# Transforms of block 1 on split operands, no idle transposes, the last product closed by token tile, and a new order with 912 pieces on another engine

## The chip, the cores and the metric

The kernel runs on one core of one Trainium2 chip. The metric is the device time of one execution in microseconds (us), as the median of several runs. TensorE (PE) multiplies; its weight loads are shown as an engine of their own (PEld). VectorE (DVE), ScalarE (ACT) and GpSimd (POOL) do the elementwise work, and SyncE (SP) issues every DMA of this kernel, one after the other in the order of the program.

## The reference

Two layers of the same two parts, on 2048 tokens of 1024 channels, with a hidden width of 3584:

```python
def _A_ref(q, k, v, shift_k, ssm_k, ssm_D):
    k_shift = sum(k_pad[:, t:t + S] * shift_k[:, ks - 1 - t] for t in range(ks))   # ks = 4
    kv = k_shift * v
    y = irfft(rfft(kv, 2 * S) * rfft(ssm_k, 2 * S))[:S]     # causal convolution, 2048 long, per channel
    return q * (y + kv * ssm_D)

def _B_ref(x, w1, b1, w2, b2):
    h = relu(x @ w1 + b1)
    return (h * h) @ w2 + b2

x = q
for _ in range(2):
    x = x + _A_ref(layernorm(x), k, v, shift_k, ssm_k, ssm_D)
    x = x + _B_ref(layernorm(x), w1, b1, w2, b2)
```

k, v and the filters are the same in both layers. So the convolution y is computed once, kept in device memory and used twice.

## The kernel before, in words

**Tiles.** The tokens are cut into four blocks of 512 (block 0 to 3), a block into four token tiles of 128; the 1024 channels are eight groups of 128. The unit of work is one layer of one block. The eight units run in the order (layer, block) = (0,0), (1,0), (0,1), (0,2), (0,3), (1,1), (1,3), (1,2), and the last four are taken two at a time as a "joint" product with seven partial products in place of eight.

**The large matmuls.** w1, relu squared and w2 make most of TensorE's work. An f32 operand is split in two halves of type fp32r: the high half is a cast by ScalarE, the low half a subtraction (operand minus high half) by VectorE or GpSimd. A product is then three matmuls (`mm3`): high by high, high by low, low by high. The weights stream from device memory: raw rows (`wr`, or `fv` and `jr` tiles), their split (`whl`, `jr`), and for weights that are used again the split form is stored once (`wd_...`) and loaded as it is.

**The convolution.** Blocks of 256 tokens are transformed with tables of cosines (`plain`, 128 by 128 pieces, and their split forms `fh`, `fl`, `ih`, `il`). Block 0's is done ahead of everything else (`first_block`, about the first 116 us). Those of blocks 1 to 3 run in the background of the first four units, as three generators that are advanced at each step of the large matmuls:

- `x_stream` shifts and multiplies K and V (`fwd_kv`), transposes and transforms the result (`fwd_x`), and writes it to device memory as `xd`;
- `g_stream` transforms the filter's rows (`fwd_g`), which come from `ssmR`, and writes `gd`;
- `prod_stream` loads both (`cx`, `cg`), multiplies them (`mult`: `cp<-cx,cg`, in pieces of 128x256 or 128x128), reduces them over the blocks (`red`: `sm<-cp`, VectorE), combines the sums (`fold`, `butterfly`: `sm<-sm`), transforms back (`fin` or `fin_plain`: results in a bank `pt`) and stores `yd`.

A block's `yd` is read when the unit of that block is prepared. For a block up to `PLAIN` the transforms are plain f32 matmuls on the whole operand; beyond it they are `mm3` on halves:

```python
        if sb <= PLAIN:                                        # fwd_x
            xt = mkfx([P, T])
            A.copy(xt, o)
        else:
            hi = mkfx([P, T], F32R)
            lo = mkfx([P, T], F32R)
            A.copy(hi, o)
            yield
            V.tensor_sub(lo, o, hi.bitcast(F32))
```

`fwd_g` does the same with the filter's rows; before, for block 1, its matmul reads the loaded tile `raw` (`fg`) directly. The inverse of block 1 takes one group of 64 channels at a time (`fin_plain`, four matmuls of 128 columns each), that of blocks 2 and 3 two groups together (`fin`: halves `yh` and `yl`, twelve matmuls of 256 columns).

**What sets the order.** Every engine call goes onto a `Tape` first. A unit of the tape is one call, or a run of TensorE calls into the same result tile; `cut(True)` starts a unit that holds all TensorE calls of a step of the large matmuls. `Tape.order` reads the table `ORDERED`, run lengths and jumps that give a permutation of all units, and `Tape.play` issues them in that order. So the recorded order of the functions above is not what runs, and each engine follows its own part of the permutation strictly. All instructions issued this way have one line in the profile: L310, in `play`. Memory is handed out in rings (`fg` 3 tiles, `fx` 4, `fk` 2, `cp` 3, `cx` and `cg` 2, `sm` 2; result banks `p1` 2, `p2` 4, `pt` 2).

**Idle transposes.** `fill(o, n)` issues n transposes of the identity into a bank whose contents are then overwritten; 40 stand at the program's start. Three further places do so: the last channel group of block 0's filter, the first transposes of block 0's tokens, and the transposes behind the normalisation between the first two units.

**The end.** The last partial product of the last joint unit runs over 14 rows p of weights; each row multiplies all four token tiles, into the banks that the names `p_...` and `pt` show at the end of the program. `j_evict` adds each bank to the accumulator (`fg<-pt,fg` and the like) and `j_store` writes it out.

Of the kernel before, what the change touches and what calls it, by code (L numbers as in the profile page):

```python
# [22 lines left out]
P = 128  # L23
# [24 lines left out]
TAIL = 0.1  # L48
LAG_RED = 2
# [25 lines left out]
PLAIN = 1  # L75
FILL = (16, 12, 4)
# [197 lines left out]
class Tape:  # L274
# [20 lines left out]
    def order(self):  # L295
        got, at = [], 0
        for t in ORDERED.split():
            n, sign, jump = re.fullmatch(r"(\d+)([-+]?)(\d*)", t).groups()
            got += range(at, at + int(n))
            at += int(n) + int(sign + (jump or "0"))  # L300
        assert sorted(got) == list(range(len(self.units)))
        return [(i, self.units[i][0]) for i in got]

    def play(self):
        def real(x):
# [2285 lines left out]
```

## Time and profile before

| | us |
|---|---|
| runs | 2574.89, 2571.48, 2575.93 |
| median | 2574.89 |
| the profiled execution's own time | 2572.81 |
| its span, first to last instruction | 2570.9 |
| TensorE busy | 2554.1 |
| weight loads (beside TensorE) | 2149.0 |
| VectorE busy | 1936.2 |
| ScalarE busy | 1139.5 |
| GpSimd busy | 1021.9 |

The granted TensorE clock is 1.000 of full speed. The program has 12184 TensorE records; a plain f32 matmul leaves two of them. All sums are made against the profiled execution's own time; the 1.9 us between it and its span lie before the first and behind the last instruction.

How to read it: a busy line gives, for each engine, the time in which it had an instruction at work. A wait is idle time of one engine ahead of an instruction, with the engine or DMA that ended it behind the arrow. A window is a stretch of the span, with each engine's busy time in it. In a timeline a row has the start, the duration, the engine, the operation with result and operands, and their shapes; an entry with x6 is six instructions of the same kind in a row, its duration that of all of them; a wait ahead of it stands in brackets at the row's end.

### The profile page before, as it was taken

What the parts mean: (1) busy time and instruction counts of PE and PEld (TensorE: products, weight loads), DVE (VectorE), ACT (ScalarE), POOL (GpSimd) and SP (SyncE); (2) the same over time, 40 slices, a digit from 0 to 9 for tenths busy, and PEclk for the clock granted to TensorE, in tenths of its full rate; (3) what the DMA queues carried; (4) which work ended last, traced back from release to release, by engine and by line L of the source; (5) the groups of instructions that cost most, each with busy time, mean ns of one, the idle gap of its engine ahead of it and who ended that gap; (6) DMA issues with size and microseconds to landing.
All of it is one profiled execution on the core that took longest, in us unless ns stands there. A gap on an engine that the chain in (4) does not pass through costs nothing.

```text
span 2570.9 us, 36794 instructions
## 1 busy us (share of the span) xinstructions
PE 2554.1 (99%) x12184; PEld 2149.0 (84%) x12184; DVE 1936.2 (75%) x3053; ACT 1139.5 (44%) x2020; POOL 1021.9 (40%) x1194
## 2 busy tenths in 40 slices
PE   9999999999999999999999999999999999999999
PEld 8988888988888888888888888888888888888887
DVE  8877998788888787878889767885778576755553
ACT  4454344534434333253322565663434566653332
POOL 4547786477573987738889100000300000003000
PEclk9999999999999999999999999999999999999999
DMA  8799999899999999899899879999988576679682
GB/s 283 262 338 336 325 302 317 323 338 381 353 329 366 339 377 337 309 305 369 336 401 371 274 264 318 329 341 383 341 301 295 169 244 225 228 266 376 212 289 82
DMA packets 405328, 792.82 MB, mean 308 GB/s; under 512 B 47505, under 2 KB 150545, under 8 KB 405138
## 3 DMA queue, kind: packets, MB, share of 16 engines
q1 hardware_dynamic: 405138, 790.47, 87.6%
q8 instruction: 96, 1.57, 0.2%
q14 instruction: 94, 0.77, 0.1%
HBM read 583.22 MB, written 207.09 MB: 307 GB/s over the span
## 4 chain that ended last, share of the span: by engine, by line
PE 90%; DMA 4%; DVE 3%; POOL 1%; issue 1%; SPq 1%; ACT 0%; DVEq 0%; POOLq 0%; ACTq 0%
PE p L310 80%; PE pt L310 11%; DMA cg<-gd 1%; DMA wd_m<-whl 1%; POOL cp L310 1%; SPq L310 1%; DVE xl L310 1%; DMA whl<-wd_m 0%; DVE whl L310 0%; DMA jr<-w 0%; DMA jr<-wd_m 0%; DMA fg<-ssmR 0%; DMA gd<-fg 0%; DMA wr<-w 0%; DVE fg L310 0%
## 5 line engine op out<-in xcount | busy, mean ns | idle before, releaser
L310 POOL TENSOR_TENSOR cp<-cx,cg 128x256 f32<-128x256 f32 (+1 forms) x864 | 683.6, 829 | 258.4 <-DVE sm L310 154.0
L310 PE MATMUL p<-xh,whl 128*128 128x512 f32 (+1 forms) x1864 | 566.2, 380 | 2.3 <-DMA whl<-wd_m 2.3
L310 POOL TENSOR_TENSOR acc<-acc,px 128x512 f32<-128x512 f32 x48 | 70.2, 1478 | 893.5 <-DMA rh<-rd 504.7
L310 PE MATMUL p<-whl,rh 128*128 128x512 f32 x1296 | 403.5, 392 | 0.3 <-DVE acc L310 0.3
L310 PEld LDWEIGHTS p<-xh,whl 128*128 128x128 f32 x1864 | 344.4, 188 | 67.0 <-issue 2.7
L310 DVE TENSOR_TENSOR whl<-wr,whl 128x512 fp32r<-128x512 f32 x387 | 299.7, 780 | 86.6 <-ACT whl L310 85.6
L310 PE MATMUL p<-xl,whl 128*128 128x512 f32 (+1 forms) x932 | 352.4, 378 | 0.1
L310 ACT CAST whl<-wr 128x512 fp32r<-128x512 f32 x405 | 246.1, 618 | 144.9 <-PE p L310 68.1
L310 PEld LDWEIGHTS p<-whl,rh 128*128 128x128 f32 x1296 | 240.2, 188 | 48.3 <-DVE acc L310 0.6
L310 DVE TENSOR_REDUCE sm<-cp 128x128 f32<-128x384 f32 (+5 forms) x288 | 249.2, 874 | 27.3 <-POOL cp L310 27.0
L310 PE MATMUL p<-whl,rl 128*128 128x512 f32 x648 | 252.7, 390 | 0.0
L310 PEld LDWEIGHTS p<-xl,whl 128*128 128x128 f32 x932 | 175.5, 188 | 31.5 <-DVE xl L310 0.3
L310 POOL TENSOR_TENSOR sm<-sm 128x256 f32<-128x256 f32 x192 | 167.8, 880 | 82.3 <-DVE sm L310 78.1
L310 ACT ACTIVATE wr<-p,b1t 128x512 f32<-128x512 f32 x130 | 89.7, 690 | 246.2 <-PE p L310 242.6
L310 DVE TENSOR_TENSOR rl<-wr,rh 128x512 fp32r<-128x512 f32 x112 | 104.2, 930 | 83.7 <-ACT rh L310 77.6
L310 PE MATMUL p<-jr,rh 128*128 128x512 f32 x496 | 154.6, 393 | 0.0
L310 PE MATMUL p<-xh,jr 128*128 128x512 f32 (+1 forms) x472 | 145.4, 379 | 0.0
L310 PEld LDWEIGHTS p<-whl,rl 128*128 128x128 f32 x648 | 121.6, 188 | 25.9
L310 DVE TENSOR_TENSOR acc<-p,acc 128x512 f32<-128x512 f32 x152 | 99.1, 684 | 52.7 <-PE p L310 52.6
L310 PE MATMUL p<-whl,xl 128*128 128x512 f32 x528 | 128.6, 389 | 0.0
L310 PE MATMUL p<-rh,whl 128*128 128x512 f32 x336 | 117.1, 389 | 0.0
L310 PE MATMUL p<-rl,whl 128*128 128x512 f32 x336 | 117.1, 389 | 0.0
(309 smaller groups left out, 5004.3 us busy)
## 6 DMA issues: line engine op xcount, KB each, us to landing
whl<-wd_m SPq DMA_DIRECT2D x231, 512.0 KB, 6.8
wr<-w SPq DMA_DIRECT2D x379, 256.0 KB, 5.7
rh<-rd SPq DMA_DIRECT2D x168, 256.0 KB, 5.5
jr<-wd_m SPq DMA_DIRECT2D x60, 512.0 KB, 6.7
rd<-acc SPq DMA_DIRECT2D x120, 256.0 KB, 4.0
wr<-td SPq DMA_DIRECT2D x112, 256.0 KB, 5.3
wd_m<-whl SPq DMA_DIRECT2D x49, 512.0 KB, 6.8
cx<-xd SPq DMA_DIRECT2D x48, 512.0 KB, 6.6
```

What stands on the lines that cost most here:

```text
L310: getattr(self.engines[e], f)(*map(real, a), **{k: real(x) for k, x in kw.items()})
```

## The change

Five things are edited.

- `PLAIN` is 0, so block 1's transforms take the paths of blocks 2 and 3: x and g on split operands, and the inverse with `fin`. The table's halves (`const_split`) are made ahead of block 1 now, and the number of ticks between two groups of x (`X_TICKS`) is that of the later blocks.
- `FILL` and its three uses are gone; the 40 transposes at the start stay.
- In the last product, the last two rows (`TAIL_ROWS`) are held back and issued by token tile: for each of the four, the six matmuls of both rows.
- `ORDERED` is another permutation.
- A second table, `SWAPPED`, names 912 units that go from VectorE to GpSimd or the other way.

```diff
+TAIL_ROWS = 2
...
-PLAIN = 1
-FILL = (16, 12, 4)
+PLAIN = 0
...
 ORDERED = (
-    "4+1 1-2 1+1 1+1 1-2 1+1 1+2 2+1 1+1 1-2 1+1 4+1 3+1 2-18 1+2 1-5 1+11 1+6 2-5 1+5 2+1 4+1 3+1 1+2 1-14 1-4 1+16 "
...
+SWAPPED = (
+    "31 3 91 6 11 101 16 67 9 42 13 13 19 4 2 23 3 5 40 5 11 29 12 2 13 27 8 4 6 7 25 2 10 10 24 8 5 9 1 6 1 30 13 "
...
         assert sorted(got) == list(range(len(self.units)))
-        return [(i, self.units[i][0]) for i in got]
+        swap, at = {}, 0
+        for n in map(int, SWAPPED.split()):
+            at += n
+            swap[at] = {"V": "G", "G": "V"}[self.units[at][0]]
+        return [(i, swap.get(i, self.units[i][0])) for i in got]
...
             def mmk(e):
-                if c == KT - 1:
-                    fill(o.t, FILL[0])
                 for r in range(2):
...
-                    for x in idle:
-                        fill(x.t, FILL[2])
-                pl.add([("PE", 600)], tr, [(ns[t], kh)], [o, *idle])
+                pl.add([("PE", 600)], tr, [(ns[t], kh)], [o])
...
                     o = ps1()
-                    if tts[n] == 2 and kh == 0:
-                        fill(o, FILL[1])
                     for c in range(4):
...
         elif k == "jb":
+            if i == 0:
+                todo_rows = []
...
-            hi, lo = (J.rt[s - jb_at][1][:, n] for n in range(2))
-            for tt in range(NT):
-                t = slice(tt * P, (tt + 1) * P)
-                mm3(os[tt], hi[:, t], lo[:, t], wh, wl, i == 0 and a in JOPEN, i == NP - 1, a not in JOPEN)
+            todo_rows.append((i, *(J.rt[s - jb_at][1][:, n] for n in range(2)), wh, wl))
+            final = u + 2 == NU and a == JORD[-1] and i >= NP - TAIL_ROWS
+            if not final or i == NP - 1:
+                for tt in range(NT):
+                    t = slice(tt * P, (tt + 1) * P)
+                    for n, hi, lo, wh, wl in todo_rows:
+                        mm3(os[tt], hi[:, t], lo[:, t], wh, wl, n == 0 and a in JOPEN, n == NP - 1, a not in JOPEN)
+                    if final:
+                        tape.cut(True)
+                todo_rows = []
             tape.cut()
```

Counted over the whole program: TensorE's matmuls and transposes go from 11768 to 11896, VectorE's instructions from 3053 to 3183, GpSimd's from 1194 to 1112, ScalarE's from 2018 to 2050, and the DMAs on SP's queue from 2434 to 2426. Of the products `cp<-cx,cg`, 309 of 128x256 and 33 of 128x128 run on VectorE now; 720 and 144 ran on GpSimd before. GpSimd has 105 low halves `whl<-wr,whl` (18 before), 33 of `jr` (6), 44 of `rl<-wr,rh` (none), 52 of `yl<-sm,yh` (none) and 23 of `fg<-fk` (none).

Three places show how the order moves. The first is VectorE in block 0, where the third group of channels is shifted (`p_544` before, `p_539` of the change, towards `fx`), while the tokens' statistics (`mv`) become a scale (`ve`, `sd`, `rs`, `rt`). Before:

```order
L310 SCALAR_TENSOR_TENSOR p_544<-xh,shkt,p_544 128x512 x2
L310 TENSOR_SCALAR ve<-mv_555 128x4
L310 RECIPROCAL rs<-sd 128x4
L310 SCALAR_TENSOR_TENSOR p_544<-xh,shkt,p_544 128x512
L310 TENSOR_TENSOR sg<-p_565,sg 128x2x4x64
L310 TENSOR_TENSOR sx<-p_539,sx 128x2x4x64
L310 TENSOR_TENSOR fx<-p_544,fx 128x512
L310 TENSOR_TENSOR sg<-sg,p_565 128x2x4x64
L310 TENSOR_TENSOR rt<-rs 128x4
```

Of the change:

```order
L438 SCALAR_TENSOR_TENSOR p_539<-xh,shkt,p_539 128x512
L438 TENSOR_TENSOR xl<-xl 128x768
L438 RECIPROCAL rs<-sd 128x4
L438 TENSOR_SCALAR ve<-mv_532 128x4
L438 SCALAR_TENSOR_TENSOR p_539<-xh,shkt,p_539 128x512
L438 TENSOR_TENSOR sg<-sg,p_561 128x2x4x64
L438 SCALAR_TENSOR_TENSOR p_539<-xh,shkt,p_539 128x512
L438 TENSOR_TENSOR sg<-p_561,sg 128x2x4x64
L438 TENSOR_TENSOR fx<-p_539,fx 128x512
L438 TENSOR_TENSOR sx<-p_538,sx 128x2x4x64
```

`fx` stands ahead of the eviction `sx` now, and `rt` and what follows from it are no longer on VectorE but on GpSimd:

```order
L438 TENSOR_TENSOR xl<-sx,sg 128x768
L438 TENSOR_TENSOR whl<-wr,whl 128x512
L438 TENSOR_TENSOR rt<-rs 128x4
L438 TENSOR_TENSOR rt<-rt,ve 128x4
L438 TENSOR_TENSOR rs<-rs,rt 128x4
L438 TENSOR_TENSOR xl<-sx,sg 128x768
```

Those rows are GpSimd's, early in block 0; ahead of them it has low halves of weights, and what moved there are the three operations of four columns.

The second place is TensorE in the first unit, at a transform of block 1's filter (`pt<-fg,...`) between the large matmuls (`p_1412`, `p_1705`, `p_1777`). Before:

```order
L310 MATMUL p_1412<-xl,whl 128x256
L310 MATMUL p_1412<-xh,whl 128x256
L310 MATMUL pt<-fg,yh 128x2x128 x4
L310 MATMUL p_1412<-xh,whl 128x256
L310 MATMUL p_1412<-xl,whl 128x256
```

Of the change:

```order
L438 MATMUL p_1705<-xl,jr 128x512
L438 MATMUL p_1705<-xh,jr 128x512
L438 MATMUL pt<-fg,fh 128x2x128 x2
L438 MATMUL pt<-fg,fl 128x2x128
L438 MATMUL pt<-fg,fh 128x2x128 x2
L438 MATMUL pt<-fg,fl 128x2x128
L438 MATMUL pt<-fg,fh 128x2x128 x2
L438 MATMUL pt<-fg,fl 128x2x128
L438 MATMUL pt<-fg,fh 128x2x128 x2
L438 MATMUL pt<-fg,fl 128x2x128
L438 MATMUL p_1777<-xh,jr 128x512
```

Four plain matmuls on the loaded rows became twelve on their halves, and they stand later: behind the large matmuls of 256 columns (two token tiles at a time), among those of 512.

The third place is TensorE at the program's end (the four token tiles' banks: two with names of their own, two called `pt`; `whl`, `jr` and `cp` are operands of the last rows). Before:

```order
L310 MATMUL p_23154<-jr,cp 128x512 x3
L310 MATMUL p_23158<-jr,cp 128x512 x3
L310 MATMUL pt<-jr,cp 128x512 x6
L310 MATMUL p_23154<-whl,cp 128x512 x3
L310 MATMUL p_23158<-whl,cp 128x512 x3
L310 MATMUL pt<-whl,cp 128x512 x6
L310 MATMUL p_23154<-whl,cp 128x512 x3
L310 MATMUL p_23158<-whl,cp 128x512 x3
L310 MATMUL pt<-whl,cp 128x512 x6
```

Of the change:

```order
L438 MATMUL p_23377<-jr,cp 128x512 x3
L438 MATMUL p_23381<-jr,cp 128x512 x3
L438 MATMUL pt<-jr,cp 128x512 x6
L438 MATMUL p_23377<-whl,cp 128x512 x6
L438 MATMUL p_23381<-whl,cp 128x512 x6
L438 MATMUL pt<-whl,cp 128x512 x12
```

The last two rows of weights go to each token tile together: six matmuls to the first bank, six to the second, twelve to the two banks `pt`.

More of the change, by code (lines that the diff above doesn't have):

```diff
@@ L125 @@
 ORDERED = (
[91 rows of a table removed]
[192 rows of a table added]
+)
+SWAPPED = (
[19 rows of a table added]
 )
@@ L1725, in tail, with tr @@
                 o = bank("p1", 2, ps1)
-                idle = [bank("p2", 4, ps2)] if t == 0 and kh else []
-                def tr(e, kh=kh, o=o, idle=idle):
+                def tr(e, kh=kh, o=o):
                     for c in range(4):
```

300 rows, old and new, of tables (ORDERED, SWAPPED) are left out of this document.

## The prediction

> **What bounds the kernel now.** I read the page's busy line first, then the list of who TensorE (PE) waited for, then the busy time by stage.
>
> ```profile
> span 2570.9 us, 36794 instructions
> ...
> PE 2554.1 (99%) x12184; PEld 2149.0 (84%) x12184; DVE 1936.2 (75%) x3053; ACT 1139.5 (44%) x2020; POOL 1021.9 (40%) x1194
> ```
>
> TensorE is busy for 2554.1 of 2570.9 us, and only 16.8 us are left in which it does nothing. So the time is TensorE's work plus a few waits, and a change is worth what it takes from either. The waits, by what ended them (total, times, longest, in us):
>
> ```profile
> PE p L310 <- DVE fx L310: 2.7, 3, 1.7
> PE p L310 <- DMA whl<-wd_m: 2.3, 1, 2.3
> PE p L310 <- ACT fg L310: 1.6, 2, 0.9
> PE p L310 <- POOL ident masks.py:199: 1.4, 1, 1.4
> PE p L310 <- ACT fx L310: 1.4, 2, 0.7
> PE pt L310 <- DMA fg<-ssmR: 1.0, 2, 0.6
> PE pt L310 <- ACT xh L310: 0.9, 1, 0.9
> ```
>
> These seven are 11.3 us; they lie in some twelve places. Most of the rest of the 16.8 us is the last store. A reader should see two things: no other engine holds the whole program up, and nothing that only reorders can gain more than about 12 us.
>
> Two stages with products beside the matmuls (columns: stretch, its length, busy us of PE, PEld, DVE, ACT and POOL, clock, DMA share, GB/s):
>
> ```profile
> 116.00:488.00 372.00, 370.97 (x1877) 316.66 (x1876) 316.59 (x504) 172.32 (x314) 234.77 (x267) 1.00 0.96 325
> ...
> 1144.00:1413.00 269.00, 266.66 (x1239) 222.61 (x1238) 227.00 (x318) 80.40 (x148) 221.13 (x278) 1.00 0.97 368
> ```
>
> Block 1's transforms run in the first of these: VectorE (DVE) is 85% busy there and GpSimd (POOL) 63%. In the last stage with products GpSimd is 82% busy, which is the nearest that any other engine comes to a bound.
>
> **The split transforms.** Block 1's 32 x transforms and 32 g transforms are plain f32 matmuls of 256 columns, and its inverse is 64 plain ones of 128 columns. In a timeline a matmul's own duration overlaps the next, so I take the distance between starts. A plain f32 matmul leaves two records.
>
> ```profile
> 11.83 1.46 PE L310 MATMUL p<-fg,yh 128*128 128x256 f32 x6
> 13.13 0.59 PE L310 MATMUL p<-fg,xh 128*128 128x256 f32 x2
> 13.56 1.03 PE L310 MATMUL p<-xh,yh 128*128 128x256 f32 x4
> ```
>
> Eight records, four matmuls, from 11.83 to 13.56: 0.433 us each for 256 columns.
>
> ```profile
> 97.39 1.95 PE L310 MATMUL pt<-xl,yh 128*128 128x128 f32 x16
> 99.17 2.89 PE L310 MATMUL p<-sx,yh 128*128 128x128 f32 x24
> ```
>
> Eight matmuls from 97.39 to 99.17: 0.2225 us each for 128 columns. The split form is already there for block 2:
>
> ```profile
> 530.90 0.40 PE L310 MATMUL pt<-fg,fh 128*128 128x256 f32 x2
> ...
> 532.34 0.63 PE L310 MATMUL p<-whl,rh 128*128 128x512 f32 x2
> ```
>
> Twelve matmuls (four products of three parts) in 1.44 us: 0.120 us each, so 0.36 us stand for 0.433. The sums: 64 x 0.433 = 27.7 us become 192 x 0.120 = 23.0 us, 4.7 us less. The inverse's 64 x 0.2225 = 14.2 us become 96 matmuls of 256 columns (two channel groups are done together), 11.5 us, 2.7 us less. Together **-7.4 us** of TensorE work, in a stage where TensorE is 99.7% busy. This is the firm term: its bounds are -7.4 and, if the time comes back as waits there, 0.
>
> What it adds lies on other engines: 16 more ScalarE casts and 16 more subtractions of 128x512 for the forward parts, and 32 casts and 32 subtractions of 128x256 for the inverse, with 16 and then 8 evictions for the products' results (8 fewer). The subtractions are some 16 x 0.7 + 32 x 0.4, about 24 us by the short forms of the rows below and 37 us at most where the engines wait for each other. The cover is VectorE's 55 us and GpSimd's 137 us of idle time in that stage; ScalarE is idle for more than half of it. The stream runs later too: in the program's order block 1's inverse moves back by some 120 us of matmuls, but its rows are read only at about 790 us. I cost it at nothing; without the cover it is the first rival.
>
> One wait goes with it. Today the matmul itself waits for the raw filter rows (fg<-ssmR, two waits, 1.0 us); now a cast and a subtraction stand between, and those have their own slack: **-1.0**, between 0 and -1.3 (a wait also costs some 0.15 us of drained pipeline).
>
> **The idle transposes.**
>
> ```profile
> 107.74 1.91 PE L310 MATMUL p<-ident 128*128 128x128 f32 x16
> 109.49 1.06 PE L310 MATMUL p<-sg,yh 128*128 128x128 f32 x8
> ```
> ```profile
> 489.36 1.47 PE L310 MATMUL p<-ident 128*128 128x128 f32 x12
> 490.66 1.04 PE L310 MATMUL p<-ident,wr 128*128 128x128 f32 x8
> ...
> 496.39 0.38 PE L310 MATMUL pt<-xh,whl 128*128 128x256 f32 x1 [0.95 <-ACT xh L310]
> ```
>
> Sixteen take 1.75 us, twelve 1.30 us, so all 32 are 3.5 us. But both groups stand ahead of a chain that VectorE and ScalarE set (normalisation, transposes, split), and TensorE still waits behind them (0.95 us at 496). Take them away and that wait grows. Bounds 0 and -3.5; nearer to 0 by the wait that is left: **-0.4**.
>
> **The order and the engines.** 912 pieces change between VectorE and GpSimd: about 340 products and 90 small sums go to VectorE, nearly 500 subtractions and additions to GpSimd. The prices:
>
> ```profile
> L310 POOL TENSOR_TENSOR cp<-cx,cg 128x256 f32<-128x256 f32 x720 | 606.0, 876 | 112.3 <-DVE sm L310 106.3 <-DMA cg<-gd 4.7 <-DVE whl L310 1.2
> ...
> L310 POOL TENSOR_TENSOR whl<-wr,whl 128x512 fp32r<-128x512 f32 x18 | 25.9, 1451 | 41.5 <-ACT whl L310 30.2 <-PE p L310 11.2
> ```
> ```profile
> L310 DVE TENSOR_TENSOR whl<-wr,whl 128x512 fp32r<-128x512 f32 x387 | 299.7, 780 | 86.6 <-ACT whl L310 85.6 <-DMA x<-acc 0.4
> ...
> L310 DVE TENSOR_TENSOR sm<-sm 128x256 f32<-128x256 f32 x40 | 17.2, 432 | 0.6
> ```
>
> No product runs on VectorE today; its nearest row is the sum of the same size, 0.432 us against 0.876. Counting pieces by their place in the program, in the first stage VectorE gets 68 products and 27 sums (41 us) and gives away 36 weight subtractions and 9 of the activations' (36 us): even. In the last stage 95 products and 24 sums leave GpSimd (104 us), some 40 us come back: 221 us become about 160. There the longest wait of all arises. The chain of waits shows before it:
>
> ```profile
> 1249.17 5.40 POOL cp L310 x8
> ```
>
> Eight products hold a buffer, the load into it waits at the head of SP's queue, and the weight load behind it lands late: TensorE stands for 2.3 us. With GpSimd at 60% that goes mostly: **-1.8**, between 0 and -2.5. In block 0 the third group of channels comes late:
>
> ```profile
> 27.59 2.31 DVE L310 TENSOR_SCALAR ve<-mv 128x4 f32<-128x4 f32 x1
> ```
> ```profile
> 32.47 0.75 PE L310 MATMUL p<-ident,fx 128*128 128x128 f32 x4 [1.72 <-DVE fx L310]
> ```
>
> A four-column VectorE operation takes 2.31 us, because GpSimd has the memory interface that both use; fx follows late. The new order puts part of this chain on GpSimd and fx before the other evictions: **-1.0**, between 0 and -1.9. Every other wait of the list I keep as it is; bounds -5 (all of them) and +8 (new ones, three or four like the longest).
>
> The Trainium skill speaks against this part: "GPSIMD Engine Reference", section 2 (Architecture), says the physical SBUF port is shared by GpSimd and VectorE. By it an exchange frees no time where both have two SBUF inputs, except by the difference of their durations. The row above agrees (2.31 us for four columns), and by the rule the 1.8 and 1.0 would be 0, the sum 2.8 less.
>
> **The last product's end.**
>
> ```profile
> 2567.19 0.69 DVE L310 TENSOR_TENSOR fg<-pt,fg 128x512 f32<-128x512 f32 x1
> 2567.24 0.33 SPq L310 DMA_DIRECT2D out<-fy  x1
> 2567.91 0.33 SPq L310 DMA_DIRECT2D out<-fg  x1
> ```
>
> Token tiles end 0.68 us apart today, as fast as VectorE adds them (0.69). With two rows taken by tile they end 1.36 us apart, but the last one ends when it did, and its addition and store follow as now. Only the store gets the queue to itself: **-0.2**, between 0 and -0.6.
>
> **The sum.** -7.4 - 1.0 - 0.4 - 1.8 - 1.0 - 0.2 = -11.8 us, from the profiled execution's own 2572.81 us (its span and 1.9 us around it): 2561.0. That execution lies 2.1 us below the median of the three runs and 1.0 below the mean of all four, so the median I expect is **2562 us**, 0.5% less.
>
> **The rivals.**
>
> 1. *The freed time comes back in block 1's stage.* The added 24 to 37 us meet a VectorE at 85%; the late halves then hold TensorE. For it: the activations' subtractions are on VectorE too, and it follows its order strictly. Against: engine exchanges keep its load even, and idle time there is 55 us. It takes back 7.4 and the small terms fail with it: about 2573. Chance 0.12.
> 2. *Slower: weights' low halves late on GpSimd.* Before, 24 weight subtractions run there, now about 150, some hundred of them while products run. Each takes 1.451 instead of 0.780 us and can stand behind a product of 0.876: 1.55 us late. TensorE needs one every 5.5 us. While the queue is short, the halves are several weights ahead and nothing shows. Where GpSimd stays behind for longer, each late half is a wait. From eleven such waits (17 us) the kernel is slower than before; with one in eight of the 125 it is 16 x 1.55 = 25 us, about 2587. For it: GpSimd at 63 to 82%. Against: its share falls where it is highest. Chance 0.07.
> 3. *More is gained:* the remaining waits go too, -5, and the idle transposes are worth half their time, -1.5: about 2554. Chance 0.11.
> 4. *The clock falls* without the idle transposes. The clock reads 1.00 in every stage, over a 2.3 us wait too; without the twelve, TensorE would stand for 0.95 + 1.30 = 2.3 us. A fall at both places, bounded by half speed over some 6 us, is 3 us each: about 2568. The skill's "TensorE: Matmul & The Clock Gate", Part 1, names an idle window of 3.4 us before the clock halves; by that rule, which no row here tests, it stays up. Chance 0.03.
>
> **Chances.** The forecast has 0.67. A measurement here can't tell less than 0.2% (5 us) from no change. Faster by more: 0.67, 0.11 and 0.03 less a little at the edge, 0.80. Within 0.2%: 0.13. Slower: 0.07. The range 2552 to 2570 runs from nearly the third rival, with most of the unknown bounds taken, to a forecast in which only the 7.4 comes and some 4 us of new waits stand against it.
>
> **What would show it.** Right: no pt<-fg,yh and pt<-fx,yh records, pt<-fg,fh at 0.120 apart before 500 us; TensorE's busy time 8 to 12 us lower; no wait for fg<-ssmR; the 2.3 us wait gone; still a wait near 107 to 115 and at about 490. Wrong: TensorE waiting for DVE or POOL whl or xl in the first stage, POOL near 90% between 500 and 800 us, a last store that ends much sooner after the last matmul, or a granted clock below 1.00.

## The result, and the profile after

| | before | after |
|---|---|---|
| median of four runs, us | 2575.07 | 2561.03 |
| lowest to highest | 2571.48 to 2575.93 | 2560.23 to 2562.63 |
| profiled execution's own time | 2572.81 | 2560.23 |
| its span | 2570.9 | 2558.5 |

The ratio is 0.9949 (0.9932 to 0.9966): 14 us less by the medians, 12.4 by the two profiled spans. 2562 with a range of 2552 to 2570 was forecast. The total came out 1 us off; some of its terms were further off, in both directions, as shown below.

The page after, span and busy time:

```profile
span 2558.5 us, 37182 instructions
...
PE 2542.8 (99%) x12184; PEld 2143.6 (84%) x12184; DVE 1984.8 (78%) x3183; ACT 1149.5 (45%) x2052; POOL 1088.3 (43%) x1112
```

TensorE is busy for 11.3 us less, and the idle rest of the span went from 16.8 to 15.7 us. VectorE has 48.6 us more and GpSimd 66.4 us more, though GpSimd lost 342 products. Whom TensorE waits for, after:

```profile
PE p L438 <- DVE xl L438: 5.4, 3, 4.2
PE p L438 <- ACT fg L438: 2.0, 2, 1.3
...
PE p L438 <- DVE fx L438: 0.8, 1, 0.8
PE pt L438 <- DVE xl L438: 0.6, 1, 0.6
```

Three entries of before are gone: the filter rows (fg<-ssmR, 1.0), the weight load (whl<-wd_m, 2.3), and most of DVE fx (2.7 to 0.8). One is new and larger than any of them: 4.2 us behind DVE xl.

Where the 12.4 us came from is read from the starts of all TensorE instructions. Each distance to the next start, less the pace of its kind (0.227 us for 512 columns, 0.119 and 0.1075 for 256 and 128, the plain ones as in the prediction), is time lost there:

| stretch | lost before, us | lost after, us |
|---|---|---|
| block 0, to the first large matmul | 11.4 | 10.4 |
| to the hand-over from the first unit to the second | 3.4 | 1.7 |
| the hand-over (some 40 us) | 2.1 | 7.2 |
| to 1100 us | 2.6 | 1.9 |
| 1100 to 1300 us | 3.7 | 0.5 |
| to the last matmul | 1.3 | 1.3 |

The lost time is 1.4 us less in all. The work at those paces is 10.9 us less: 7.5 from the transforms and 3.4 from the 32 idle transposes. From the last matmul's start to the span's end it is 4.22 before and 4.17 after.

### The profile page after: what moved, and what is told of

It is laid out like the page before. It is cut to its first block, busy times and chain, and to the rows that moved or that the text cites. A ratio compares the mean times of both kernels' runs of the same rounds, so it can differ in the third digit from the quotient of the medians.

```text
span 2558.5 us, 37182 instructions
## 1 busy us (share of the span) xinstructions
PE 2542.8 (99%) x12184; PEld 2143.6 (84%) x12184; DVE 1984.8 (78%) x3183; ACT 1149.5 (45%) x2052; POOL 1088.3 (43%) x1112
## 4 chain that ended last, share of the span: by engine, by line
PE 95%; DVE 2%; DMA 1%; issue 1%; POOL 0%; ACT 0%; SPq 0%; DVEq 0%; POOLq 0%; ACTq 0%
PE p L438 84%; PE pt L438 11%; DVE sm L438 0%; DVE xl L438 0%; DMA wd_m<-whl 0%; DVE cp L438 0%; DVE p L438 0%; DMA px<-b 0%; DMA cg<-gd 0%; POOL cp L438 0%; DMA yh<-inv 0%; DVE whl L438 0%; DVE fx L438 0%; DVE acc L438 0%; DVE st L438 0%
## 5 line engine op out<-in xcount | busy, mean ns | idle before, releaser
L438 POOL TENSOR_TENSOR cp<-cx,cg 128x256 f32<-128x256 f32 (+1 forms) x522 | 421.4, 834 | 133.3 <-DMA cg<-gd 68.4
L438 DVE TENSOR_TENSOR whl<-wr,whl 128x512 fp32r<-128x512 f32 x300 | 233.8, 785 | 86.2 <-ACT whl L438 83.9
L438 DVE TENSOR_TENSOR cp<-cx,cg 128x256 f32<-128x256 f32 (+1 forms) x342 | 257.7, 799 | 11.3 <-DMA cg<-gd 10.3
L438 POOL TENSOR_TENSOR whl<-wr,whl 128x512 fp32r<-128x512 f32 x105 | 150.0, 1433 | 108.2 <-ACT whl L438 80.9
L438 POOL TENSOR_TENSOR wr<-wr 128x512 f32<-128x512 f32 x10 | 13.9, 1394 | 387.5 <-DVE acc L438 383.5
```

Of the source, the lines that this page charges most:

```text
L438: getattr(self.engines[e], f)(*map(real, a), **{k: real(x) for k, x in kw.items()})
```

## The experiments

Times are medians; e1 to e4 ran beside a before of 2573.89, e5 to e8 beside 2573.81, e9 and e10 beside 2574.34. Unless an edit says "before", it is made in the changed kernel.

### The transforms

```diff
-                    mm3(ou, fh[:, 2 * e + r], fl[:, 2 * e + r], hi[:, q_], lo[:, q_], True, True)
+                    if sb == 1:
+                        PE.matmul(ou, fh[:, 2 * e + r].bitcast(F32), hi[:, q_].bitcast(F32), start=True, stop=True)
+                    else: ...   # the same in fwd_g and, with two matmuls for each half, in inverse
```

> The changed kernel, with block 1's transforms as plain f32 matmuls again (the high halves of tables and operands taken as f32; the casts and subtractions stay, and what the low halves add is left out). Theory: the split is worth its work on TensorE, 64 x 0.433 - 192 x 0.119 = 4.9 us for x and g, 32 x 0.433 - 96 x 0.120 = 2.3 us for the inverse: 7.2 us slower than the change, about 2568. Rival: the time freed there came back as waits, or the gain came from the order alone: within 2 us of the change, about 2561 to 2563.

2570.77, ratio to before 0.9987 (0.9978 to 0.9996): 9.7 us slower than the change. In the timeline of TensorE, the same group of the filter's transforms, split in the change and plain in e1:

```profile
142.94 0.40 PE L438 MATMUL pt<-fg,fh 128*128 128x256 f32 x2
...
144.37 0.40 PE L438 MATMUL p<-xh,jr 128*128 128x512 f32 x1
```
```profile
143.00 1.89 PE L438 MATMUL pt<-fg,fh 128*128 128x256 f32 x8
144.53 0.58 PE L438 MATMUL p<-xh,jr 128*128 128x512 f32 x1
144.95 0.40 PE L438 MATMUL p<-xl,jr 128*128 128x512 f32 x1
```

Twelve split matmuls take 1.43 us. Four plain ones take 1.53, and the next start comes 0.42 later instead of 0.23: 1.73 in all, four times 0.433. So the plain price also sits in the instruction behind the group, and a sum over the group's own rows misses a tenth of it. By the spans e1 is 10.5 us slower; some 3.2 of it are new waits elsewhere (1.1 us on an eviction at 720, 0.8 on fx at 1071), and 7.3 are work at the paces above. The theory's 7.2 holds for the work. That some 3 us of waits come with it suggests that the order fits the pace of the TensorE that it was made for; no run isolates this.

### The new wait at the hand-over

TensorE and ScalarE of the change at this place, and the chain of waits that ends there:

```profile
479.79 1.12 PE L438 MATMUL p<-ident,wr 128*128 128x128 f32 x4 [4.24 <-DVE xl L438]
...
481.14 0.63 PE L438 MATMUL pt<-xh,whl 128*128 128x256 f32 x2
481.56 0.41 PE L438 MATMUL pt<-xl,whl 128*128 128x256 f32 x1
```
```profile
477.80 0.62 ACT L438 CAST whl<-wr 128x512 fp32r<-128x512 f32 x1 [5.09 <-DMA wd_m<-whl]
478.32 0.58 ACT L438 CAST xh<-p 128x512 fp32r<-128x512 f32 x1
```
```profile
468.89 8.56 DMA wd_m<-whl
477.45 0.03 ACTq L438
```

The list of waits names DVE xl, but VectorE had nothing to do. ScalarE stands for 5.09 us in front of a weight's cast, since the buffer it writes to is still being stored; the cast of the activations (xh) is queued behind it, and xl behind that. The store was issued at 468.89 and took 8.56 us. And when TensorE starts again its matmuls of 256 columns are 0.21 us apart instead of 0.12 (two from 481.14 to 481.56): half the clock, until 484.8. That costs another 2.3 us.

The experiment moves this one store ahead of four loads in SP's order.

```diff
         assert sorted(got) == list(range(len(self.units)))
+        for i, j in ((2186, 2154),):        # the store; the load of wr that it now follows
+            got.remove(i)
+            got.insert(got.index(j) + 1, i)
```

> The changed kernel with one DMA moved in SP's order: the store of a split weight (wd_m<-whl) that is issued at 468.89 us goes ahead of four loads, to about 464. Theory: ScalarE's cast into that store's buffer waits 5.1 us for it and holds the casts xh behind it, and this makes TensorE's 4.24 us wait at the hand-over from the first unit to the second; the clock falls behind it. With the store landed by about 471 the wait shrinks to 1 to 1.5 us, no half-speed rows follow, and the kernel is 4.5 to 5.5 us faster than the change: about 2556. Rival: the idle transposes that were taken away are the cause, the chain of normalisation needs that time: TensorE's wait stays at 2.3 us or more, and the kernel is at most 2 to 3 us faster.

2556.38 (2555.97 to 2556.93), ratio to before 0.9928 (0.9915 to 0.9940): 4.65 us faster than the change, and the fastest kernel of this study but for e10, which is level with it. SP and ScalarE there:

```profile
463.04 0.38 SPq L441 DMA_DIRECT2D wd_m<-whl  x1
```
```profile
472.49 0.62 ACT L441 CAST whl<-wr 128x512 fp32r<-128x512 f32 x1 [0.64 <-DMA wr<-w]
473.02 0.58 ACT L441 CAST xh<-p 128x512 fp32r<-128x512 f32 x1
```

The cast waits 0.64 us, no wait of TensorE above 0.2 us is left there, no half-speed rows follow, and the time lost at the hand-over is 0.9 us instead of 7.2. So the store's place caused it. Of these 6.3 us only part reaches the time, since e2 loses 2.8 us more than the change at smaller waits after 500 us (0.6 of it on a weight at 1314). Moving the cast itself behind the xh casts was not tried.

### The idle transposes

```diff
                     o = ps1()
+                    if tts[n] == 2 and kh == 0:
+                        fill(o, 12)
```

> The changed kernel with the twelve idle transposes put back at the hand-over from the first unit to the second (1.3 us). Theory: they run inside the time in which TensorE waits for the store, the wait goes from 4.24 to 2.9 us, which leaves the clock up (2.3 us were lost by half speed behind it): 2.3 us faster than the change, about 2558.7. Rival: the clock falls all the same, or the fills delay what stands behind them: within 0.5 us of the change or up to 1.3 slower.

2561.63, ratio to before 0.9953 (0.9940 to 0.9966): no difference to the change's 0.9949. The transposes run inside the wait, as expected, and it is shorter:

```profile
470.47 1.47 PE L438 MATMUL p<-ident 128*128 128x128 f32 x12
...
479.03 1.05 PE L438 MATMUL p<-ident,wr 128*128 128x128 f32 x4 [3.17 <-DVE xl L438]
...
480.31 0.63 PE L438 MATMUL pt<-xh,whl 128*128 128x256 f32 x2
480.73 0.41 PE L438 MATMUL pt<-xl,whl 128*128 128x256 f32 x1
```

But the clock falls behind 3.17 us as well, for 3.4 us of time. The theory's step, that a wait of 2.9 us leaves the clock up, was wrong: in e7 the clock also fell at a wait of 2.86 us, and the last section shows what decides it. The fall in the change does not come from the missing transposes, since it is there with them too.

The same twelve taken out of the kernel before (`FILL = (16, 0, 4)`):

> The kernel before, without the twelve idle transposes at the hand-over from the first unit to the second (1.3 us). Theory, the prediction's: TensorE waits behind them for VectorE and ScalarE anyway, and the wait at 496 us grows from 0.95 to about 2.2 us: within 0.3 us of before. Rival 1: they delay the transposes behind them: up to 1.3 us faster. Rival 2: the clock falls behind the longer wait, as it did in the change behind 3.2 and 4.2 us: 1 to 3 us slower.

2573.63, ratio 1.0003 (0.9994 to 1.0011): the same. In e8's timeline the waits ahead of the second unit:

```profile
490.31 1.09 PE L310 MATMUL p<-ident,wr 128*128 128x128 f32 x8 [0.81 <-ACT wr L310]
...
496.17 0.38 PE L310 MATMUL pt<-xh,whl 128*128 128x256 f32 x1 [0.91 <-ACT xh L310]
```

A new wait of 0.81 us stands in their place, and the lost time at the hand-over grows by 1.1 us where 1.3 of transposes went. It grew elsewhere than expected (the wait at 496 stayed), but as much. Here the prediction's reasoning holds.

In block 0 it does not. First the sixteen put back into the change (`fill(o.t, 16)` ahead of the last channel group's matmuls), then the sixteen taken out of before (`FILL = (0, 12, 4)`):

> The changed kernel with the sixteen idle transposes put back in block 0 (1.7 us). Theory: the waits behind that place are 0.65 us longer in the change than before, so only so much of the fills was cover: the kernel gets 1.1 us slower than the change (0.9 to 1.8), about 2562.1. Rival, the prediction's own term: the waits behind them grow by nearly all that the fills took, so putting them back costs 0 to 0.3.

> The kernel before, without the sixteen idle transposes in block 0 (1.75 us). Theory, from their return in the changed kernel, which cost 1.6 us there: they stood on TensorE's path, and the first large matmul starts 1.3 to 1.8 us earlier: 2572 to 2572.6 where before has 2573.8. Rival, the prediction's term: they covered the wait for the chain of VectorE and ScalarE behind them, which now grows by nearly as much: within 0.4 us.

e4: 2563.09, ratio to before 0.9959 (0.9946 to 0.9971). By the medians that is 2.1 us slower than the change, which the spread of its runs (2561.83 to 2569.61) leaves unclear, so the reading rests on the trace: the first large matmul starts 1.6 us later, counted from the first wait of the program. Of TensorE in the change and in e4:

```profile
106.14 1.16 PE L438 MATMUL p<-sg,yh 128*128 128x128 f32 x8 [1.31 <-ACT fg L438]
...
110.13 0.66 PE L438 MATMUL p<-ident,cp 128*128 128x128 f32 x4 [0.61 <-DVE xl L438]
```
```profile
106.30 1.97 PE L438 MATMUL p<-ident 128*128 128x128 f32 x16 [1.02 <-ACT fg L438]
...
111.89 0.66 PE L438 MATMUL p<-ident,cp 128*128 128x128 f32 x4 [0.96 <-DVE xl L438]
```

The waits behind them do not shrink. The one shown grows from 0.61 to 0.96, and a pause of some 0.3 us inside the eight transposes ahead of it goes in turn; from start to start both kernels lose 1.1 us there. The rows give the reading: the sixteen stand ahead of transforms (p<-sg,yh) from which the chain that is waited for afterwards starts, so they push it back too. e9: 2570.49, ratio 0.9986 (0.9977 to 0.9995). From the end of the wait near 106.8 to the first large matmul it takes 7.13 us instead of 8.13. So block 0's sixteen were worth 1.0 to 1.6 us by the traces, not nothing. The lower end of e9's interval, 1.3 us, lies above the rival's 0.4; its median is 3.9 us faster, more than the theory's 1.2 to 1.8, and what the rest of it is was not found.

### The exchange of engines

```diff
-        return [(i, swap.get(i, self.units[i][0])) for i in got]
+        return [(i, self.units[i][0]) for i in got]                       # e5, on top of e2
+        return [(i, self.units[i][0] if 5005 <= i <= 6097 else swap.get(i, self.units[i][0])) for i in got]   # e6, on top of e2
```

> The kernel with the store moved (2556.4), but none of the 912 pieces exchanged: every piece on the engine on which it was recorded, the order of the change kept. Theory: the exchange of engines carries the terms of the order (the 2.3 us wait of the last stage with products, the late fx in block 0): GpSimd is back at 80% or more of the stage from 1130 to 1400 us, a weight load waits there again, and low halves, products and sums come late where the order counted on the other engine: 3 to 10 us slower, 2559 to 2566. Rival: the new permutation alone did it, the engines do not matter while TensorE is 99% busy: within 1 us.

> The kernel with the store moved (2556.4), with the 163 exchanged pieces of the last stage with products alone (about 1135 to 1400 us; 97 products among them) back on their recorded engines. Theory: GpSimd goes from 66% of that stage to 80% or more, as before the change, the products hold cg and cx longer and TensorE stands for 2 to 3 us more in that stage: 2558 to 2560. Rival: the wait at 1264 us was one of the old order's, the new one keeps it away with GpSimd as full: within 0.5 us.

e5: 2603.48, ratio 1.0116 (1.0100 to 1.0131), 47 us slower than e2. e6: 2567.52, ratio 0.9977 (0.9968 to 0.9986), 11.1 us slower. The direction is the theory's, the sizes are several times larger. In e5 TensorE waits most for fx (12.9 us) and fg (7.1), and once 5.1 us for a weight; GpSimd is at 73% of the stretch from 1150 to 1420 us, not at the theory's 80%. For e6, the last stage's window (columns as in the prediction), then what SP waited for in it:

```profile
1135.00:1405.00 270.00, 261.89 (x1210) 217.75 (x1209) 215.07 (x302) 78.89 (x146) 221.88 (x276) 0.99 0.96 357
```
```profile
SPq L441 <- POOL cp L441: 57.6, 19, 7.3
```
```profile
1203.33 1.22 PE L441 MATMUL p<-whl,rh 128*128 128x512 f32 x2 [4.98 <-DMA whl<-wd_m]
```

GpSimd is at 82% again, SP stands up to 7.3 us at a time in front of loads whose buffers GpSimd's products hold, and a weight load behind one of them is 5 us late. The clock is at half for 6.8 us from 1202.4 on, and another wait, 2.6 us on fx, follows at 1224. In the stage before and after the change, SP's waits on products were:

```profile
SPq L310 <- POOL cp L310: 43.0, 19, 4.7
```
```profile
SPq L438 <- DVE cp L438: 47.2, 16, 5.8
...
SPq L438 <- POOL cp L438: 19.2, 13, 2.5
```

and the change's own window over that stage is

```profile
1144.00:1413.00 269.00, 269.00 (x1260) 225.59 (x1259) 251.95 (x390) 83.21 (x153) 177.90 (x206) 1.00 0.99 369
```

GpSimd is at 177.9 of 269 us (about 160 were forecast). But the queue is not freed: SP waits longer for products than before, 66.4 us against 43.0. What went is the weight load that lands late behind such a wait: whl<-wd_m no longer stands in TensorE's list. With that order but the old engines the waits fall elsewhere and hit a weight. This also limits what e5 and e6 say: they price the exchange within an order made for it. What another order with the old engines would give is open; before itself is one, with 2574.

### The price of a product on VectorE

```diff
-            pr = cv.tile([P, CU, j + 1], F32, name="cp", bufs=3)
+            pr = cv.tile([P, j + 1, CU], F32, name="cp", bufs=3)
...
-                G.tensor_mul(pr[:, :, a:e].rearrange("p c i -> p i c"), xt[:, a:e],
+                G.tensor_mul(pr[:, a:e], xt[:, a:e],
...
-            V.tensor_reduce(sm[:, ty, jj], st["pr"], axis=AX.X, op=OP.add)
+            V.tensor_reduce(sm[:, ty, jj], st["pr"].rearrange("p i c -> p c i"), axis=AX.X, op=OP.add)
```

> The kernel with the store moved (2556.4), with the products cp<-cx,cg written in a row instead of with a stride (and read with the stride by the reduction). In the change a product of 128x256 takes VectorE 0.818 us (0.64 where GpSimd does nothing), not the 0.432 of the sum of the same size that the prediction used. Theory: the stride of the write costs the difference: VectorE's products fall to about 0.43 to 0.5 us and the reductions, which read with the stride, stay near 0.87; VectorE is some 60 us less busy, and the time moves by less than 1.5 us, since VectorE's load is hidden. Rival: two operands from memory make the price, and GpSimd at work beside them: the products stay at 0.64 or more.

The groups of products and of the longest reductions, in the change and in e7:

```profile
L438 DVE TENSOR_TENSOR cp<-cx,cg 128x256 f32<-128x256 f32 x309 | 240.6, 818 | 8.8 <-DMA cg<-gd 8.2 <-DVE yl L438 0.4
...
L438 DVE TENSOR_REDUCE sm<-cp 128x128 f32<-128x1024 f32 x48 | 57.6, 1201 | 3.0 <-POOL cp L438 2.9
```
```profile
L441 DVE TENSOR_TENSOR cp<-cx,cg 128x256 f32<-128x256 f32 x309 | 175.9, 587 | 4.5 <-DMA cg<-gd 4.2
...
L441 DVE TENSOR_REDUCE sm<-cp 128x128 f32<-128x1024 f32 x48 | 95.9, 1998 | 0.8 <-POOL cp L441 0.6
```

2608.62, ratio 1.0139 (1.0125 to 1.0152), 52 us slower than e2. The product's half of the theory holds: products that meet no work of GpSimd take 0.416 us in a row and 0.643 with the stride. Beside GpSimd's work they still take 0.71 on average, and that is the rival's part. The other half is wrong: the reductions pay more than the products save (2.0 us instead of 1.2 for the longest), VectorE is 87 us busier by the page (2073.9 instead of 1987.2), and that is not hidden. TensorE loses 49 us more from start to start, 22 of them in waits on fx, acc, yl and yh. In e2 VectorE is at 88 to 93% of each stage between 116 and 1405 us; there it has little room.

### Two more waits

```diff
+        for i, j in ((2186, 2154), (3222, 3214), (4295, 4305)):    # the last two: a reduction behind the evictions
```

> The kernel with the store moved (2556.4), with two reductions of VectorE (0.94 us at 702.6 and 1.07 us at 958.4) moved behind the evictions of the banks for which TensorE waits there (0.31 and 0.61 us). Theory: a wait on an eviction is worth what stands ahead of it in VectorE's order: both waits go, 0.9 us faster, 2555.5. Rival: the reductions are then late for what follows them, and as much comes back: within 0.3 us of 2556.4 or slower.

2556.27 (2554.20 to 2558.38), ratio 0.9929 (0.9916 to 0.9941): level with e2. Both waits are gone, and at 1414 us TensorE now waits 1.75 us for yh where it waited 0.25. The rival is right as to the sum; that the two moves caused the later wait was not shown.

## Why the prediction was right, and where not

| term of the sum | forecast, us | found, us |
|---|---|---|
| split transforms | -7.4 | -7.5 (starts), 7.3 of e1's 10.5 |
| filter's rows | -1.0 | -1.4 (0.58 and 0.77 us of lost time, both gone) |
| idle transposes, block 0 | -0.4 for all 32 | -1.0 to -1.6 for sixteen (e4, e9); the four others, 0.4 us of work, not tried |
| idle transposes, hand-over | in the -0.4 | no difference seen (e8), nor in the new order (e3) |
| wait at 1264 us | -1.8 | -2.5, and 0.6 at 1140 to 1150 |
| block 0's fx | -1.0 | -0.8 to -1.5: block 0 is 3.15 us shorter, 0.2 of it ahead of the first wait; twenty transposes are 2.15 of the rest by their work, 1.4 to 2.0 by e4 and e9 |
| last product's end | -0.2 | -0.05 |
| the hand-over's new wait | none | +5.1 of lost time |

The filter's rows, block 0's fx and the last product's end are read from the starts alone; no run tried them by themselves.

The reading that carried the forecast held: TensorE is the bound, so its own work counts in full where it is 99.7% busy, and the split's price could be taken from block 2's rows. The largest term was right to 0.1 us, and rival 1 (it comes back in that stage) did not occur: the stage lost less time than before. One count was off without effect: x's casts take the place of copies that were there before, so ScalarE's new casts for the forward parts are 8 and not 16.

**The idle transposes** were mis-sized in block 0. The step "both groups stand ahead of a chain that VectorE and ScalarE set, and TensorE still waits behind them" was true of the place and wrong as a reason: in block 0 the transposes delayed TensorE's own part of that chain. A wait behind a filler says only that the filler could be cover. Whether it is, depends on whether what the wait waits for starts ahead of the filler or behind it.

**The hand-over** was the miss. "Every other wait of the list I keep as it is", with up to +8 for new ones: one came, 4.2 us with 2.3 us of half clock behind it, and ate more than the filter and the 1264 us terms together brought. Its cause is not one of the rivals'. It is the order itself: a store placed late in SP's queue. Net of the 1.3 us of transposes that left, the hand-over costs 3.8 us. The total stood because other places gave more than their terms: block 0 some 2 us, 1100 to 1300 us 1.3, the filter's rows and the stretch to 1100 us 1.2 together. That these make up for the hand-over is luck: no term of the sum stood for its wait, nor for these surpluses. Two of the signs named for being wrong did show, a wait for xl at the first stage's end and a granted clock of 0.998, and they mark this place.

**The wait at 1264 us** went, and e6, with that stage's exchange undone, has one like it again. But the step "with GpSimd at 60% that goes mostly" is not the whole cause: GpSimd's share fell from 82 to 66%, yet SP waited longer for products than before. What e6 shows is the chain (product, buffer, load, weight), not that a lower share by itself ends it; how the new order keeps the weights out of that chain stays open.

**The product's price on VectorE** was taken from a sum of the same size, 0.432 us; it is 0.818. The sum writes its result in a row, the product writes with a stride, and 205 of the 309 products meet work of GpSimd, beside which they take 0.91 us on average. The stage sums of VectorE were too low by 25 to 40 us (68 and 97 products). It did not reach the result as far as the list of waits shows: no product stands in it.

**The port rule of the Trainium skill** ("GPSIMD Engine Reference", section 2, a port shared by GpSimd and VectorE) would have made the gain 2.8 us smaller. The runs agree with the sharing (a product takes 0.91 us beside GpSimd's work and 0.643 without), but the exchange gained all the same: without it this order loses 47 us.

**Rival 4, the clock,** had 0.03 and did happen, at one of its two places, behind a longer wait than it assumed and for less than its 3 us. It did not come from the missing transposes, since e3 has it too. That the clock stayed up over the 2.3 us wait of before was luck of where the wait lay in time (see the last section): at the same place it fell in e8 (1.81 us) and in e9 (2.27 us). The Trainium skill's idle window of 3.4 us ("TensorE: Matmul & The Clock Gate", Part 1) does not agree as a length of wait that is needed, since the clock fell behind 3.17 us in e3 and behind 1.81 in e8; as the length of a step it does, as the last section shows.

Rivals 2 and 3 did not occur: no weight's low half shows among the waits, and the remaining waits did not go.

## What to carry to other kernels

Where one engine is 99% busy, price a change by that engine's own work first, from start to start and with the instruction behind the group; it was the large term that came out to 0.1 us. Then look at every place where the order moves, one queue at a time, for an instruction that stands behind something late: a cast that waits for a store's buffer holds everything behind it, and the list of waits will name the last link (here VectorE) instead of the store. A filler in front of a wait is free only if what the wait waits for does not itself stand behind the filler.

## What the runs showed of the hardware

The clock fell to half behind each of the seven waits of TensorE of 3.08 us or more in these runs (3.08, 3.17, 3.99, 4.24, 4.98, 5.12, 5.99), for 3.4 or 6.8 us. Behind shorter ones it sometimes did. The wait at 1264 us in e8 and in before:

```profile
1262.36 0.47 PE L310 MATMUL p<-xh,whl 128*128 128x512 f32 x1 [1.81 <-DMA whl<-wd_m]
...
1264.12 1.05 PE L310 MATMUL p<-xh,whl 128*128 128x512 f32 x2
1264.97 0.63 PE L310 MATMUL p<-xl,whl 128*128 128x512 f32 x1
```
```profile
1264.40 0.47 PE L310 MATMUL p<-xh,whl 128*128 128x512 f32 x1 [2.33 <-DMA whl<-wd_m]
...
1264.93 0.61 PE L310 MATMUL p<-xh,whl 128*128 128x512 f32 x2
1265.39 0.39 PE L310 MATMUL p<-xl,whl 128*128 128x512 f32 x1
```

After 1.81 us two matmuls take 0.85 from start to the next start (half speed), after 2.33 us 0.46 (full). So the length alone does not decide below 3 us. The traces show what does. In all twelve the granted clock changes only on a grid: within a run the changes lie whole multiples of 3.413 us apart, to 5 ns, and it stays at half for one such step or two. Cut into these steps, the same two stretches read (columns as in the prediction; e8, then before):

```profile
1259.50:1262.91 3.41, 1.59 (x8) 1.04 (x7) 2.79 (x4) 0.64 (x2) 3.33 (x4) 1.00 1.06 393
1262.91:1266.32 3.41, 3.41 (x10) 2.65 (x9) 2.03 (x4) 2.25 (x4) 3.41 (x7) 0.50 1.02 416
```
```profile
1260.05:1263.46 3.41, 2.01 (x9) 1.32 (x8) 2.98 (x3) 1.71 (x3) 3.41 (x4) 1.00 1.05 396
1263.46:1266.87 3.41, 2.47 (x11) 2.10 (x12) 2.62 (x4) 2.05 (x5) 3.33 (x6) 1.00 1.04 415
```

The 1.81 us of e8 lie in one step, in which TensorE was idle for 1.82 of 3.41 us; the next step ran at half clock. The 2.33 us of before lie across a boundary, 1.40 us idle in one step and 0.94 in the next, and the clock stayed up. Over the twelve traces all 18 falls ahead of the last matmul follow a step with 1.82 us idle or more. Of the steps at full clock, none with 1.75 us idle or less has a fall behind it, and one with 1.91 (in e5) has none either. So what counts in these runs is the idle time within a step of the grid, about half of it, and a wait's place on the grid decides. The Trainium skill ("TensorE: Matmul & The Clock Gate", Part 1) says of its window that it runs freely, without regard to the program; these rows agree, with a step of 3.413 us.

A stride costs VectorE about as much for each element on the reading side as on the writing side: a product of 128x256 took 0.643 us with a strided write and 0.416 without (no GpSimd work beside it), a reduction of 1024 elements 2.0 us with a strided read and 1.2 without. In the change the product with the strided write takes 0.91 us beside GpSimd's work; the reduction, which reads one operand, takes 1.20 with or without it.
